# Sliding-window attention and MLP: splitting the W1 cast over two engines, centring rows without scaling in group 0, pacing GpSimd casts, spreading weight differences

## The chip, the cores and the metric

The kernel runs on one core of a Trainium2 chip. The metric is the device time of one launch in microseconds (us), as the median of several executions. A profile of one execution goes with each kernel; its span is about 2 us shorter than the measured time. Engine names in the profile: PE is TensorE (matmuls), PEld its weight loads, DVE is VectorE, ACT is ScalarE, POOL is GpSimd. "Lnnn" is a line of that kernel's own source, so the same operation has different line numbers before and after.

## The reference, cut to what matters

```python
def _attn_ref(q, k, v):                       # (8, 8, 576, 64), float32
    scores = (1 / sqrt(D)) * q @ k^T          # keys i-63 .. i of each query i only (window 64, causal)
    attn = softmax(scores)
    return attn @ v

def _moe_ref(x, g_ln, w_ch1, w_ch2):          # x: the attention result as (8, 576, 512)
    mu, var = mean(x), mean((x - mu)**2)      # over the 512 columns
    xn = (x - mu) / sqrt(var + 1e-06) * g_ln
    return x + relu(xn @ w_ch1) @ w_ch2       # 512 -> 2048 -> 512
```

## The kernel before

There are nine groups. Group g (0 to 7) is the first 512 rows of batch g; group 8 is the last 64 rows ("tails") of all eight batches. The MLP of group g is cut into about 30 "units" of TensorE work. After each unit the program emits what is listed for that slot: pieces of the attention of batch g+1 (scores, mask, product with v, row statistics, normalised rows z and their transpose zT), and the loads and casts of batch g+2. The order of emission is each engine's order of execution, so `at(u, f, ...)` sets where in each engine's queue the piece stands, but not when it runs.

GpSimd casts the inputs from fp32 to fp16. It has no data dependence on the MLP, so it runs a cast as soon as the input has landed and what stands before it in GpSimd's queue is done:

```python
    def cast_qk(b, half):
        for x in range(2):                    # q, then k: two casts of 128x1024 back to back
            ...
            nc.gpsimd.tensor_copy(out=dst..., in_=t...)
    def cast_v(b, c0, c1):
        nc.gpsimd.tensor_copy(out=vA[b][:, c0:c1, :, 0:D], in_=v32[b][:, c0:c1])
    def w1_cast(i):                           # 16 casts of 128x512 in all, g_ln folded in
        for c in range(2):
            nc.gpsimd.tensor_scalar(out=w1g[...], in0=t[:, c], scalar1=g4[:, kc:kc + 1], ..., op0=ALU.mult)
```

On VectorE, among others, are the mask, the normalised rows and the operands of layer 2, which from group 1 on is done by a scheme of seven block products instead of eight. It needs sums of activations in every group (`sw`) and eight differences of weights (`tw`, and two in place in `w2s`), which are computed once:

```python
    def s_mask(g, j):                         # two SBUF inputs, 128x1024
        nc.vector.tensor_tensor(out=ptv, in0=ptv, in1=mb, op=ALU.mult)
    def z_step(g, kb):                        # one SBUF input, fp32 -> fp16
        nc.vector.tensor_scalar(out=z, in0=x_norm..., scalar1=mv[:, 0:1], scalar2=rs[:, 0:1],
                                op0=ALU.subtract, op1=ALU.mult)
    def t_weights(i, c):                      # two SBUF inputs, 128x1024
        nc.vector.tensor_tensor(out=o, in0=a, in1=b, op=ALU.subtract)
```

The slots that matter here:

```python
        if g == 0:
            for n, i in enumerate((1, 2, 4)):           # six weight differences at the end of group 0
                for c in range(2):
                    at(26 + 2 * n + c, t_weights, i, c)
        else:
            if g == 1:
                at(0, t_weights, 3, 0); at(0, t_weights, 3, 1)      # (two lines in the source)
            ...
        if g > 1 and b < B:                             # attention of the next batch, b = g + 1
            for j in range(4):
                at(1 + 6 * j, s_mm, b, j); at(2 + 6 * j, s_mask, b, j)
                bz(7 + 6 * j, b, j); at(min(13 + 6 * j, 28), zt_step, b, j)
        if 0 < g and b + 1 < B:                         # loads and casts of the batch after it
            ...
            at(e + 8, cast_qk, n, 0)
            at(e + 10, cast_qk, n, 1)
            at(e + 16, cast_v, n, 0, 4)
```

The softmax here doesn't subtract the row's maximum and nothing guards it: scores larger than these inputs give would overflow.

## Time and profile before

The time is 346.97 us (346.14 to 348.06), the span of the profile 344.8 us. The table gives the stages. A stage begins at the first layer-1 matmul of its group in the timeline of PE, and the last one ends with the span. Busy time and granted clock are from the view of windows.

| stage before | from, us | length, us | PE busy, us | PEclk |
|---|---|---|---|---|
| start, to the first MLP matmul | 0 | 23.63 | | |
| group 0, layer 1 | 23.63 | 25.40 | 18.91 | 0.89 |
| group 0, layer 2 | 49.03 | 21.30 | 20.58 | 1.00 |
| group 1 | 70.33 | 49.40 | 38.53 | 0.90 |
| groups 2 to 5 | 119.73 | 127.93 | 123.41 | 1.00 |
| group 6 | 247.66 | 36.05 | 32.57 | 1.00 |
| group 7 | 283.71 | 29.59 | 29.59 | 1.00 |
| group 8 | 313.30 | 31.50 | 26.37 | 0.98 |

TensorE bounds the kernel nearly everywhere, so what counts is where PE waits. This is the view of PE's waits of the kernel before; the columns are: who waited <- for whom, us in total, times, longest.

```profile
PE hph L424 <- ACT hrT L429: 7.4, 1, 7.4
PE tp L216 <- POOL qk L126: 5.9, 2, 3.4
PE ztp L341 <- DVE z L330: 5.0, 8, 2.0
...
PE xps L307 <- DVE pt L291: 2.9, 3, 1.0
...
PE hph L424 <- POOL w1g L187: 2.1, 2, 1.3
```

The first line is one stall at the boundary of groups 0 and 1. The second contains one of 3.44 us in group 0: PE transposes q of batch 1, whose cast stands behind the W1 casts in GpSimd's queue. The timeline of GpSimd shows these (start, duration, engine, line, operation, tiles, shapes, count):

```profile
17.32 12.51 POOL L187 TENSOR_SCALAR w1g<-w1s,g 128x512 f16<-128x512 f32 x8 [0.77 <-DMA w1s<-in_moe_w_ch_dram]
29.82 12.34 POOL L187 TENSOR_SCALAR w1g<-w2s,g 128x512 f16<-128x512 f32 x8
42.11 2.01 POOL L126 CAST qk<-qk 128x1024 f16<-128x1024 f32 x2
```

The first wait of the list and the one for `pt` (the product with v waits for the mask, 2.9 us) have another cause, which two timelines show together. VectorE before:

```profile
69.76 6.08 DVE L371 TENSOR_TENSOR tw<-w2s,tw 128x1024 f16<-128x1024 f16 x3
...
186.70 5.05 DVE L291 TENSOR_TENSOR pt<-pt,mask 128x1024 f16<-128x1024 f16 x1 [2.64 <-ACT pt L278]
...
194.09 0.66 DVE L291 TENSOR_TENSOR pt<-pt,mask 128x1024 f16<-128x1024 f16 x1
```

GpSimd before, at the same times:

```profile
70.11 3.98 POOL L126 CAST qk<-qk 128x1024 f16<-128x1024 f32 x4
...
186.06 1.05 POOL L123 CAST qk<-qk 128x1024 f16<-128x1024 f32 x1
...
188.27 1.03 POOL L123 CAST qk<-qk 128x1024 f16<-128x1024 f32 x1
...
189.31 1.88 POOL L145 CAST vA<-v 128x2048 f16<-128x2048 f32 x1
```

The same mask multiplication takes 0.66 us at 194.09 and 5.05 us at 186.70, and the long one ends at 191.75, 0.56 us after the last cast that reads SBUF (189.31 + 1.88 = 191.19). Three weight differences take 6.08 us across the casts of 70.11. Operations with an input in PSUM keep their duration: all seven `xn` that overlap such a cast take 0.69 us, like the other 29. This is what the Trainium skill describes in "SBUF — State Buffer", section "Who interferes with whom": VectorE with two SBUF inputs and a GpSimd instruction that reads SBUF want the same read port, and the one that comes second stands still until the other is done. The mask before shows it with 5.05 us instead of 0.66.

### The profile page before, as it was taken

The page shows a single profiled execution, that of the slowest core. Times are in us where ns is not written, and L with a number is a line of the kernel's source. Part 1 is how long each engine was busy: PE and PEld are TensorE (multiplying, and loading weights), DVE is VectorE, ACT ScalarE, POOL GpSimd, SP SyncE. Part 2 cuts the span into 40 slices and gives each one's busy share as a digit, 9 for nine tenths or more (in the row PEclk, how much of TensorE's full clock was granted, in tenths as well). Part 3 has the DMA queues.
Part 4 walks back from the last instruction along what each step waited for, and adds up shares of the span by engine and source line. Part 5 has one row for each costly group of instructions (what it writes and reads, how often), then busy time and mean ns, then how long its engine had stood idle before and what let it go on. Part 6 is the DMA issues. An engine that isn't in the chain of part 4 may idle for free.

```text
span 344.8 us, 7486 instructions
## 1 busy us (share of the span) xinstructions
PE 306.4 (89%) x3093; PEld 201.3 (58%) x3093; DVE 228.0 (66%) x366; ACT 170.5 (49%) x340; POOL 120.2 (35%) x152
## 2 busy tenths in 40 slices
PE   4976699928979899998999899899999789999993
PEld 1545354416867745854684478358746664586483
DVE  0662066497789668859885897689558974872352
ACT  2484442504856477246536652673387227813600
POOL 6599985456340180046007300800223303001000
PEclk9989989976999999999999999999999999999999
DMA  8999449997199479939975894794197995003004
GB/s 181 281 381 267 172 145 283 308 195 234 41 224 231 110 179 223 204 124 154 238 155 167 167 243 96 190 184 72 64 209 141 153 195 131 2 2 122 0 2 122
DMA packets 119890, 56.82 MB, mean 165 GB/s; under 512 B 96080, under 2 KB 112976, under 8 KB 119856
## 3 DMA queue, kind: packets, MB, share of 16 engines
q1 hardware_dynamic: 115904, 45.10, 58.3%
q0 software_dynamic: 2976, 10.72, 9.8%
q10 hardware_dynamic: 976, 0.53, 0.6%
q8 instruction: 24, 0.39, 0.5%
q14 instruction: 10, 0.08, 0.1%
HBM read 38.80 MB, written 9.44 MB: 140 GB/s over the span
## 4 chain that ended last, share of the span: by engine, by line
PE 58%; DVE 17%; POOL 9%; DMA 6%; SPq 3%; ACT 3%; issue 2%; DVEq 0%; POOLq 0%
PE hps L393 24%; PE wX L464 13%; POOL w1g L187 6%; PE wZ L464 5%; DVE pt L291 5%; PE hph L424 4%; PE wY L464 4%; DMA qk<-in_k_dram 3%; PE xps L307 3%; PE sc L274 2%; DVE osb L481 2%; DVE sw L383 2%; SPq L139 2%; PE ztp L341 2%; DVE stats L315 2%
## 5 line engine op out<-in xcount | busy, mean ns | idle before, releaser
L393 PE MATMUL hps<-zT,w1g 128*128 128x512 f16 x480 | 111.3, 381 | 0.7 <-ACT zT L344 0.7
L397 ACT ACTIVATE hrT<-hps 128x512 f16<-128x512 f32 x120 | 71.8, 598 | 38.7 <-PE hps L393 37.3
L393 PEld LDWEIGHTS <-w1g 128*128 128x128 f16 x480 | 45.4, 98 | 53.6 <-issue 4.5
L354 POOL DMA_DIRECT2D out_dram<-osb x18 | 12.6, 697 | 154.0 <-DVE osb L481 143.5
L464 PEld LDWEIGHTS <-sw 128*128 128x128 f16 x512 | 48.7, 98 | 10.0 <-issue 3.2
L291 DVE TENSOR_TENSOR pt<-pt,mask 128x1024 f16<-128x1024 f16 x28 | 37.0, 1320 | 19.3 <-ACT pt L278 10.6
L344 ACT COPY zT<-ztp 128x512 f16<-128x512 f16 x36 | 20.9, 582 | 42.7 <-PE ztp L341 42.7
L464 PEld LDWEIGHTS <-hrT 128*128 128x128 f16 x384 | 37.1, 98 | 6.4 <-issue 0.7
L424 PE MATMUL hph<-zT,w1g 128*128 128x256 f16 x192 | 26.3, 291 | 10.4 <-ACT hrT L429 7.4
L383 DVE TENSOR_TENSOR sw<-hrT 128x1024 f16<-128x1024 f16 x32 | 22.7, 712 | 15.5 <-ACT hrT L397 15.5
L323 ACT ACTIVATE rs<-mv,epst 128x1 f32<-128x1 f32 x36 | 10.6, 295 | 38.4 <-DVE mv L317 38.4
L126 POOL CAST qk<-qk 128x1024 f16<-128x1024 f32 x24 | 25.0, 1050 | 9.1 <-PE tp L216 2.8
L424 PEld LDWEIGHTS <-w1g 128*128 128x128 f16 x192 | 19.0, 103 | 14.7 <-issue 8.6
L284 ACT ACTIVATE pt<-sc 128x512 f16<-128x512 f32 x40 | 21.7, 595 | 9.1 <-PE sc L274 8.2
L315 DVE BATCH_NORM_STATS2 stats<-xn 128x6 f32<-128x512 f32 x36 | 25.0, 695 | 1.2
L210 DVE COPY qkT<-tp 128x1024 f16<-128x1024 f16 x6 | 7.3, 1225 | 27.9 <-PE tp L216 27.9
L313 DVE TENSOR_TENSOR xn<-xps,rcp 128x512 f32<-128x512 f32 x36 | 24.9, 691 | 1.2
L481 DVE TENSOR_TENSOR osb<-wX,xn 128x512 f32<-128x512 f32 (+1 forms) x25 | 16.6, 664 | 11.1 <-PE wX L464 11.1
L330 DVE TENSOR_SCALAR z<-xn,mv,rs 128x512 f16<-128x512 f32 x36 | 21.3, 593 | 3.2 <-ACT rs L324 3.0
L145 POOL CAST vA<-v 128x512 f16<-128x512 f32 (+1 forms) x14 | 16.8, 1210 | 9.9 <-DMA v<-in_v_dram 9.7
L307 PEld LDWEIGHTS <-pt 128*64 128x64 f16 x576 | 12.5, 112 | 12.9 <-DVE pt L291 4.8
L429 ACT ACTIVATE hrT<-hph 128x512 f16<-128x512 f32 x24 | 14.3, 597 | 11.0 <-PE hph L424 10.9
(70 smaller groups left out, 445.7 us busy)
## 6 DMA issues: line engine op xcount, KB each, us to landing
qk<-in_q_dram SPq DMA_DIRECT2D x16, 512.0 KB, 6.2
v<-in_v_dram SPq DMA_DIRECT2D x32, 256.0 KB, 5.7
out_dram<-osb POOLq DMA_DIRECT2D x14, 512.0 KB, 3.2
w2s<-in_moe_w_ch_dram SPq DMA_DIRECT2D x12, 512.0 KB, 6.4
qk<-in_k_dram SPq DMA_DIRECT2D x8, 512.0 KB, 6.6
qk<-in_k_dram SPq DMA_DIRECT2D x16, 256.0 KB, 6.5
w1s<-in_moe_w_ch_dram SPq DMA_DIRECT2D x4, 512.0 KB, 6.6
tk<-in_k_dram SPq DMA_DIRECT2D x8, 256.0 KB, 4.3
```

Source lines behind the costliest of these rows:

```text
L126: nc.gpsimd.tensor_copy(out=dst[:, :].rearrange("p (a j) e d -> p a e j d", j=j), in_=t[:, :].rearrange("p (a e j d) -> p a e j d", e=2, j ...
L284: nc.scalar.activation(out=pt[:, par], in_=sc[par], func=AF.Exp, bias=0.0, scale=scale)
L291: nc.vector.tensor_tensor(out=ptv, in0=ptv, in1=mb, op=ALU.mult)
L307: nc.tensor.matmul(out=xps[64 * r:64 * r + 64, h, :D + 1], lhsT=pt[:, par, hp, r, :], rhs=rhs, start=True, stop=True)
L313: nc.vector.tensor_tensor(out=xn, in0=xps[:, :, 0:D], in1=rcp_b, op=ALU.mult)
L315: nc.vector.bn_stats(out=stats, in_=xn.rearrange("p h d -> p (h d)"))
L383: nc.vector.tensor_tensor(out=S[i], in0=a, in1=b, op=op)
L393: nc.tensor.matmul(out=hps, lhsT=w1g[:, kc, 128 * hc:128 * (hc + 1)], rhs=zT[g][:, kc, :], start=(kc == 0), stop=(kc == NKC - 1),)
L397: nc.scalar.activation(out=hrT[:, hc, :], in_=hps, func=AF.Relu, bias=0.0, scale=1.0)
L424: nc.tensor.matmul(out=hps[:, e], lhsT=w1g[:, kc, 128 * hc:128 * (hc + 1)], rhs=zT[g][:, kc, 256 * half:256 * half + 256], start=(kc == 0) ...
L464: nc.tensor.matmul(out=xyz[bank][:, t], lhsT=lhsT, rhs=rhs, start=bool(first and t == 0 and hc == 0), stop=(t == 1 and hc == 7), skip_grou ...
L481: nc.vector.tensor_tensor(out=o, in0=xyz[bank][:, ts], in1=x if base == "x" else o, op=ALU.add)
```

## The change

Its intent has five main parts.

1. Of the 16 W1 casts, GpSimd keeps 8 and ScalarE takes 8, so that GpSimd gets to the casts of batch 1 sooner.
2. Group 0 uses rows that are centred but not scaled by r = 1/sqrt(var + eps). As r is positive, relu(r·a) = r·relu(a), so r can be multiplied in at the end, in the addition to the output (`add_out`). That takes the ScalarE steps for r (`r_step`) off the path to the first MLP unit.
3. The eight weight differences move from the group boundary to one slot each in units 1 to 8 of group 1.
4. From group 2 on, each GpSimd cast is preceded by a tiny copy of one element per partition that reads a result of MLP unit u, or, for v, of the next batch's normalisation (the "pace" token), so that casts come one at a time, and the mask is emitted where no cast should be running. Scores, masks and tails get new slots.
5. In group 1, the shifted copy of v (`vB`) of batch 2 is made by two DMAs instead of by seven VectorE copies.

The diff holds more: layer 1 takes its four input chunks in the order 0, 2, 1, 3 (first those whose weights GpSimd casts), the casts of W2 and the loads after them are emitted only at unit 6 of group 0, the first blocks of group 0 are normalised and transposed in another order, and the casts of the tails are cut into three paced pieces.

The diff, cut to its core:

```diff
-    def w1_cast(i):
+    def w1_cast(i, c):
...
-            nc.gpsimd.tensor_scalar(out=w1g..., in0=t[:, c], scalar1=g4[:, kc:kc + 1], ..., op0=ALU.mult)
+        if c == 0:
+            nc.gpsimd.tensor_scalar(out=dst, in0=t[:, c], scalar1=g4[:, kc:kc + 1], scalar2=None, op0=ALU.mult)
+        else:
+            nc.scalar.activation(out=dst, in_=t[:, c], func=AF.Identity, bias=0.0, scale=g4[:, kc:kc + 1])
...
     def z_step(g, kb):
+        if g == 0:
+            nc.vector.tensor_scalar(out=z, in0=x, scalar1=mv[:, 0:1], scalar2=None, op0=ALU.subtract)
+        else: ...
+    def pace(t):
+        nc.gpsimd.tensor_copy(out=tok, in_=t)
...
         def add_out(kb):
-            nc.vector.tensor_tensor(out=o, in0=ch[kb], in1=x_norm..., op=ALU.add)
+            nc.vector.scalar_tensor_tensor(out=o, in0=ch[kb], scalar=rss[(g, kb)][:, 0:1],
+                in1=x_norm..., op0=ALU.mult, op1=ALU.add)
...
     TAILS = {
-        6: (... (10, s_mm, 8, 0), (11, s_mask, 8, 0), (16, b_step, 8, 0), (22, zt_step, 8, 0), ...
+        6: (... (11, s_mm, 8, 0), (12, s_mask, 8, 0), (17, b_step, 8, 0), (23, zt_step, 8, 0), ...
...
         if g == 1:
-            at(4, init_vB, 2)
+            at(4, alloc_vB, 2)
             at(5, cast_v, 2, 0, 4)
+            at(5, make_vB, 2)
-            for c in range(4):
-                at(7, vB_cur, 2, c, 1)
-                if c < 3:
-                    at(7, vB_prev, 2, c, 1)
...
-                at(0, t_weights, 3, 0)
-                at(0, t_weights, 3, 1)
+                for n, i in enumerate((1, 2, 4, 3)):
+                    for c in range(2):
+                        at(1 + 2 * n + c, t_weights, i, c)
...
             for j in range(4):
-                at(1 + 6 * j, s_mm, b, j)
-                at(2 + 6 * j, s_mask, b, j)
-                bz(7 + 6 * j, b, j)
-                at(min(13 + 6 * j, 28), zt_step, b, j)
+                at((0, 6, 11, 17)[j], s_mm, b, j)
+                at((1, 7, 12, 18)[j], s_mask, b, j)
+                bz((6, 11, 17, 23)[j], b, j)
+                at((12, 17, 23, 28)[j], zt_step, b, j)
...
+            if n < NPE:                       # batches 2 and 3 (cast in groups 0 and 1): as before, not paced
+                at(e + 8, cast_qk, n, 0)
+                at(e + 10, cast_qk, n, 1)
+                ...
+            else:
+                for u, x, half in ((3, 0, 0), (5, 1, 0), (8, 0, 1), (10, 1, 1)):
+                    at(u, lambda u=u: pace(hrTs[g][:, u, 0:1]))
+                    at(u, cast_q, n, x, half)
+                ...
+                for u, c, j in ((18, 0, 1), (20, 1, 2), (24, 2, 2), (26, 3, 3)):
+                    at(u, ... pace(...))
+                    at(u, cast_v, n, c, c + 1)
```

## The prediction

> **What bounds the kernel now.** TensorE: PE is busy 306.4 of the 344.8 us span (busy table), so about 38 us of PE idle is all there is to win, and some 15 us of it lies in the first 22 us (inputs arriving) and the last 5 us (stores), which the change hardly touches. The waits and the timeline of PE put the rest in four places.
>
> 1. Start, group 0. GpSimd casts W1 from 17.3 to 42.1 us: 16 casts of 1.56 us (timeline of GpSimd). PE waits 0.85 + 1.26 us for W1, 0.94 us for the zT copy, 3.44 us (39.6 to 43.2) for the q cast queued behind W1, and then runs at a lower granted clock (0.86).
> 2. Boundary of groups 0 and 1. Three weight differences on VectorE take 6.08 us from 69.8 (one alone 4.88, normally 0.68), because GpSimd casts q and k from 70.1 to 74.1. They delay the normalisation, ScalarE waits 8.36 us for its variance, PE waits 7.36 us. Granted clock afterwards 0.68 to 0.81.
> 3. Groups 2 to 5, period 32.24 us. The first mask multiply takes 4.0 to 5.05 us (0.69 elsewhere), until the GpSimd casts end (186.7 to 191.75 against 185.1 to 191.1). PE waits 0.98 us for it and 0.40 us for z at the end of each group.
> 4. Group 6 (36.1 us): waits of 2.28, 0.74 and 0.42 us.
>
> The Trainium skill, "SBUF — State Buffer", section "Who interferes with whom", says a VectorE instruction with two SBUF inputs contends with a GpSimd instruction that reads SBUF, and the later one fully blocks. The trace agrees: mask and weight differences stretch until the casts end, while operations with a PSUM input keep their 0.69 us.
>
> **What the change does, costed.**
> - W1: GpSimd keeps 8 casts (12.5 us, done near 30), ScalarE gets 8 at about 0.6 us each (its 128x512 passes take 0.58 to 0.60). ScalarE then limits the first eight MLP units (relu 0.6 + cast 0.6 against 0.87 of PE), so layer 1's second part starts only 1 to 2 us earlier; the 3.44 us stall and its cold clock vanish. Gain about 6.5 us.
> - Unscaled rows remove a 0.6 us wait per block at the start, which ScalarE's casts take back. About 0.
> - Weight differences spread: the 7.36 us stall and the cold clock after it vanish. Gain 8 us. One difference can still be caught by the casts (about 1 us, little on PE).
> - Pacing: one cast blocks VectorE for at most about 1 us, and the mask runs before the first cast. Gain 1.4 us x 4 groups, less new collisions: 5 us.
> - Tails in group 6: gain 2 to 3 us.
> The 2 us wait in group 1 (98.3 to 103, v cast against sums) isn't addressed.
>
> Sum: about 22 us, nearly all on PE's path. Predicted 324.5 us, 8 in 10 between 319 and 332. Chances: faster by over 2% 0.95, within 2% 0.04, slower 0.01.
>
> **What would show each step right.** GpSimd's last W1 cast ends near 30 us; no PE wait of 3 us on a q cast; layer 2 of group 0 starts near 42 to 43 us (49.0 before). No PE wait over 2 us at the group 0 to 1 boundary. Period of groups 3 to 5 near 31 us, no mask multiply over 1.8 us. Group 6 near 33.5 us.
>
> **What would make it wrong.** W2 and the next q, k, v arriving late, so that group 0 is limited by DMA; ScalarE's casts delaying its relus more than said; paced v casts delaying the vB copies; paced casts colliding with the pre-sums, so that periods stay near 32 us.

## The result, and the profile after

The changed kernel takes 331.71 us (330.8 to 332.5, four runs) against 346.97 us (346.14 to 348.06, four runs): ratio 0.956, 95% interval 0.952 to 0.960. Ratios here are the mean time of one kernel's fast runs over that of the other's of the same rounds, so not quite the ratio of the medians quoted. The time lies just inside the predicted range, but the gain is 15.2 us where 22 were expected. The stages, by the same definition as above:

| stage | before | after | difference | predicted |
|---|---|---|---|---|
| start | 23.63 | 21.95 | -1.68 | (in the next line) |
| group 0, layer 1 | 25.40 | 19.95 | -5.45 | -6.5 with the start |
| group 0, layer 2 | 21.30 | 21.28 | 0.0 | 0 |
| group 1 | 49.40 | 45.65 | -3.75 | -8 |
| groups 2 to 5 | 127.93 | 123.83 | -4.10 | -5 |
| group 6 | 36.05 | 34.98 | -1.07 | -2 to -3 |
| group 7 | 29.59 | 30.03 | +0.44 | 0 |
| group 8 | 31.50 | 32.03 | +0.53 | 0 |
| span | 344.8 | 329.7 | -15.1 | about -22 |

The view of PE's waits after:

```profile
PE tp L221 <- DVE qkT L215: 2.7, 1, 2.7
PE ztp L356 <- DVE z L342: 2.7, 4, 1.1
PE tp L221 <- POOL qk L131: 2.3, 1, 2.3
...
PE hph L440 <- ACT zT L359: 1.5, 1, 1.5
PE xps L312 <- DVE xn L318: 1.4, 1, 1.4
```

The 7.4 us wait and the wait for W1 are gone, and so is the wait of 3.4 us for a cast of q (what is left of that line, 2.3 us, is at the very start, while inputs arrive). The new head of the list is a single wait of 2.7 us in group 1. W1 in GpSimd's timeline after:

```profile
17.38 3.11 POOL L193 TENSOR_SCALAR w1g<-w1s,g 128x512 f16<-128x512 f32 x2 [0.79 <-DMA w1s<-in_moe_w_ch_dram]
21.60 3.27 POOL L193 TENSOR_SCALAR w1g<-w1s,g 128x512 f16<-128x512 f32 x2 [1.11 <-DMA w1s<-in_moe_w_ch_dram]
24.84 6.18 POOL L193 TENSOR_SCALAR w1g<-w2s,g 128x512 f16<-128x512 f32 x4
```

GpSimd is through with W1 at 31.0 instead of 42.2 us, and layer 2 of group 0 starts at 41.9 instead of 49.0. Each cast on ScalarE takes 0.71 to 0.72 us (0.6 had been estimated from passes that read PSUM).

Group 1 is where the prediction missed most. VectorE after:

```profile
64.89 2.10 DVE L342 TENSOR_SCALAR z<-xn,mv,rs 128x512 f16<-128x512 f32 x1
...
70.44 2.22 DVE L386 TENSOR_TENSOR tw<-w2s 128x1024 f16<-128x1024 f16 x1
72.59 0.58 DVE L342 TENSOR_SCALAR z<-xn,mv,rs 128x512 f16<-128x512 f32 x1
73.10 2.94 DVE L386 TENSOR_TENSOR tw<-w2s,tw 128x1024 f16<-128x1024 f16 x1
75.96 1.21 DVE L215 COPY qkT<-tp 128x1024 f16<-128x1024 f16 x1
...
142.47 0.69 DVE L296 TENSOR_TENSOR pt<-pt,mask 128x1024 f16<-128x1024 f16 x1 [1.84 <-ACT pt L283]
```

GpSimd after, at the same times:

```profile
62.19 3.98 POOL L131 CAST qk<-qk 128x1024 f16<-128x1024 f32 x4
...
70.23 1.89 POOL L150 CAST vA<-v 128x2048 f16<-128x2048 f32 x1 [2.39 <-DMA v<-in_v_dram]
...
73.47 2.02 POOL L131 CAST qk<-qk 128x1024 f16<-128x1024 f32 x2
...
144.71 0.70 POOL L348 CAST tok<-hrT 128x1 f32<-128x1 f16 x1 [2.73 <-ACT hrT L412]
145.35 1.04 POOL L131 CAST qk<-qk 128x1024 f16<-128x1024 f32 x1
```

One difference is held by the cast of v of batch 2 (until 72.1), another by the casts of q and k of batch 3 (until 75.5). The second one starts 0.37 us before these casts, while GpSimd still issues the DMAs of `vB` (72.42 to 73.47), so which of the two engines came first can't be read from this profile. Neither is a collision at the old place, the boundary; the spread operations met other casts, which are not paced. The copy `qkT`, which only reads PSUM and itself keeps its 1.21 us, stands behind the 2.94 us difference in VectorE's queue, and PE waits for that copy. PE after:

```profile
77.23 1.01 PE L221 MATMUL tp<-ident,qk 128*128 128x128 f16 x8 [2.73 <-DVE qkT L215]
78.03 3.82 PE L440 MATMUL hph<-zT,w1g 128*128 128x256 f16 x24
```

The 24 `hph` matmuls after the wait take 3.82 us, where the same 24 take 2.80 us in a run without it (pace_q3 below). The view of windows says why, in its column for the granted clock (0.50, then 0.81, after PE stood still; asked for 76.72 to 80.14 alone it gives 0.50):

```profile
77.20:79.00 1.80, 1.77 (x13) 1.52 (x13) 1.80 (x4) 0.72 (x1) 0.69 (x1) 0.50 1.08 171
79.00:82.00 3.00, 3.00 (x36) 2.29 (x35) 2.02 (x2) 1.60 (x4) 1.06 (x2) 0.81 0.96 154
```

(columns: window; its length, then busy us and instructions of PE, PEld, DVE, ACT, POOL; granted clock as a share of full speed; DMA share; GB/s).

In groups 3 to 5 the period is 30.97 us, as predicted; the first mask takes 0.69 us (142.47 above) and its cast waits for the token at 144.71. PE is busy for 123.20 of the 123.83 us of groups 2 to 5, 99.5%, so there is nothing more to win there by moving waits.

### The profile page after: what moved, and what is told of

Same layout as the page of the kernel before. It is cut to its first block, busy times and chain, and to the rows that moved or that the text cites. A ratio compares the mean times of both kernels' runs of the same rounds, so it can differ in the third digit from the quotient of the medians.

```text
span 329.7 us, 7565 instructions
## 1 busy us (share of the span) xinstructions
PE 303.8 (92%) x3093; PEld 200.2 (61%) x3093; DVE 206.5 (63%) x359; ACT 175.1 (53%) x348; POOL 127.2 (39%) x198
## 4 chain that ended last, share of the span: by engine, by line
PE 71%; DVE 12%; ACT 11%; issue 2%; DMA 2%; POOL 0%; DVEq 0%
PE hps L408 28%; PE wX L480 15%; PE wZ L480 8%; PE wY L480 3%; PE sc L279 3%; PE xps L312 3%; ACT pt L289 3%; PE hph L440 2%; DVE sw L398 2%; PE ch L420 2%; PE ztp L356 2%; ACT hrT L412 2%; DVE stats L320 2%; DVE xn L318 2%; PE tp L221 2%
## 5 line engine op out<-in xcount | busy, mean ns | idle before, releaser
L398 DVE TENSOR_TENSOR sw<-hrT 128x1024 f16<-128x1024 f16 x32 | 23.6, 741 | 21.2 <-ACT hrT L412 21.2
L296 DVE TENSOR_TENSOR pt<-pt,mask 128x1024 f16<-128x1024 f16 x28 | 19.7, 705 | 15.1 <-ACT pt L289 7.7
L315 DVE RECIPROCAL rcp<-xps 128x8 f32<-128x8 f32 x36 | 7.4, 205 | 26.8 <-PE xps L312 26.8
L348 POOL CAST tok<-hrT 128x1 f32<-128x1 f16 x25 | 10.1, 403 | 34.3 <-ACT hrT L412 29.9
L150 POOL CAST vA<-v 128x512 f16<-128x512 f32 (+1 forms) x26 | 19.3, 744 | 9.9 <-DMA v<-in_v_dram 9.7
L342 DVE TENSOR_SCALAR z<-xn,mv,rs 128x512 f16<-128x512 f32 x32 | 20.1, 632 | 0.8 <-ACT rs L332 0.6
```

Source lines behind the costliest of these rows:

```text
L342: nc.vector.tensor_scalar(out=z, in0=x, scalar1=mv[:, 0:1], scalar2=rss[(g, kb)][:, 0:1], op0=ALU.subtract, op1=ALU.mult)
L398: nc.vector.tensor_tensor(out=S[i], in0=a, in1=b, op=op)
```

## The experiments

All kernels gave correct results. Runs are in three sessions, each on a chip of its own and with its own runs of the kernel before (medians 348.04, 347.99 and 348.52 us); between sessions compare the ratios. Every one of these kernels is faster than the kernel before by over 2%, except e5 and e7, where the interval reaches across 2% and the verdict is unclear. e1 to e4 were profiled twice: the times read from timelines below are of the first profile, and where the kept second one differs it is given too. The changed kernel was run again as a control (c_after). Where an expectation names a theory by a letter, A is the blocking of VectorE by GpSimd casts that are not paced, B is that VectorE simply has too much work in group 1, C is that the tail block and batch 7 share units in group 6, and D the rivals of C.

### Control: the changed kernel again (c_after)

No edit.

> The changed kernel itself again, as a control on the same chip as the runs beside it. The first experiments showed group 1 at 41.4 us in one kernel and 45.7 us in another although both have the same code there, so one profile of group 1 is not a fixed number. If that is so (when the loads of v and of the next q and k land decides which weight difference meets which GpSimd cast), the runs of this kernel scatter over 3 us or more, around 330 to 333 us; if the kernel is steady, they agree within 1 us and group 1 is again 45.5 us.

Measured: 331.92 us, ratio 0.952 (0.947 to 0.956); its fast runs spread from 329.33 to 333.15, and one of 334.61 was counted as slow and left out (it is over 1.5% above the fastest, but its granted clock, 0.981, isn't below that of the others, 0.981 to 0.989, so it may belong to the same scatter). In the profile group 1 takes 46.36 us, with a PE wait of 3.96 us for the same copy. What follows: the runs scatter by over 3 us, as the first alternative says. The kernel before scatters as much in the same session (347.01 to 350.77, eleven runs), so this isn't new with the change, and a difference of 1 to 2 us between single runs means nothing here.

### Group 1: pacing the casts of batch 3 (e1_pace_q3)

```diff
-                at(e + 8, cast_qk, n, 0)
-                at(e + 10, cast_qk, n, 1)
+                for u, x, half in ((9, 0, 0), (11, 1, 0), (13, 0, 1), (15, 1, 1)):
+                    at(u, lambda u=u: pace(hrTs[g][:, 2 * (u % 8), 256 * (u // 8):256 * (u // 8) + 1]))
+                    at(u, cast_q, n, x, half)
```

> Edit: in group 1 alone, the four GpSimd casts of batch 3's q and k are paced to MLP units 9, 11, 13 and 15, instead of running as soon as GpSimd is free. Theory A (contention: the spread weight differences of group 1 wait out unpaced GpSimd casts that read SBUF, and the qkT copy behind them in VectorE's queue holds up PE): the third weight difference falls from 2.94 us to about 0.7, PE's 2.73 us wait for the qkT copy and the cold clock after it vanish, group 1 falls from 45.65 us to about 41.5 to 42.5, the time to about 328 us. Rival B (VectorE simply has 5.4 us more work ahead of that copy, so its queue is late whatever GpSimd does): the wait stays near 2.7 us, the time within 1 us of 331.7.

Measured: 328.74 us (328.3 to 329.06), ratio 0.944 (0.940 to 0.948). PE's wait for the copy falls from 2.73 to 0.31 us and the clock stays up (24 `hph` matmuls in 2.80 us). But group 1 only falls to 44.53 us (43.60 in the second profile), not to the expected 41.5 to 42.5: the cast of v of batch 3, now right after the paced casts (86.34, 2.16 us), holds a pre-sum for 2.51 us, and PE waits 1.77 us for a later pre-sum of the same queue and 1.13 us for a z. So the wait did come from the unpaced casts of q and k, and the next unpaced cast took its place.

### Group 1: the delayed copy on ScalarE instead (e2_copy_on_act)

```diff
-            at(4, t_main, 2, 0, 1, 1)
+            at(4, t_main, 2, 0, 1, 0)
```

> Edit: the third copy of transposed q out of PSUM in group 1 is made by ScalarE instead of VectorE; the GpSimd casts stay unpaced. Theory A's chain (blocked difference, then copy behind it, then PE): the difference stays at about 2.9 us, but PE no longer waits 2.73 us for the copy; group 1 gains 2 to 4 us, the time is about 328.5 to 330 us. If PE's wait came from somewhere else (late q cast, z of block 3), the wait of about 2.7 us stays and the time does not move by 1 us.

Measured: 328.17 us (326.96 to 329.44), ratio 0.943 (0.939 to 0.947); group 1 43.71 us (43.52 in the second profile). The difference is still blocked (2.94 us), but PE no longer waits for the copy. A wait of 2.54 us for a z appears later, behind a mask of 2.23 us that runs against the cast of v (84.05 to 85.94). What follows: the way the time reaches PE is the place of the copy in VectorE's queue; and again a later cast takes some of it back.

### Group 1: the differences back at the boundary (e3_weights_back)

```diff
+        if g == 0:
+            for n, i in enumerate((1, 2, 4)):
+                for c in range(2):
+                    at(26 + 2 * n + c, t_weights, i, c)
...
-                for n, i in enumerate((1, 2, 4, 3)):
-                    for c in range(2):
-                        at(1 + 2 * n + c, t_weights, i, c)
+                at(0, t_weights, 3, 0)
+                at(0, t_weights, 3, 1)
```

> Edit: the eight weight differences are put back where the kernel before has them (six at the end of group 0, two at the start of group 1); all else is as changed. Theory A: the 7 us PE stall at the boundary of groups 0 and 1 comes back, while group 1's new 2.7 us wait goes: group 1 is again about 48 to 50 us against 45.65, the time about 335 to 336 us. Rival (the gain of group 1 came from the vB copies that moved to DMA, not from spreading): the time stays within 1 us of 331.7.

Measured: 332.8 us (331.9 to 333.47), ratio 0.956 (0.952 to 0.960), against 0.956 and 0.952 of the changed kernel in its two sessions. The stall at the boundary is back (three differences in 6.08 us, PE waits 6.13 us), yet group 1 takes 47.04 us (46.03 in the second profile) against 45.65 and 46.36, and the time is near that of the rival and not the 335 to 336 us of theory A. So spreading the differences, which had been credited with 8 us, is by itself worth 0 to 1.5 us by these figures (the intervals of the ratios leave up to some 3.5 us open): it exchanged one collision for others. The other 2.4 to 3.4 us by which group 1 is shorter than the 49.40 us before are not traced to a part of the change; the rival's own reason, the `vB` copies, is tested in e10 below and finds no support.

### Group 1 cleared of casts (e9_g1_clear)

The casts of batch 2 move ahead (units 27 and 28 of group 0), the v cast of batch 2 waits until the differences are through, and all casts of batch 3 are paced.

```diff
-            at(30, cast_qk, 2, 0)
-            at(30, cast_qk, 2, 1)
+            at(27, cast_qk, 2, 0)
+            at(28, cast_qk, 2, 1)
...
-            at(5, cast_v, 2, 0, 4)
-            at(5, make_vB, 2)
+            at(7, lambda: pace(hrTs[1][:, 14, 0:1]))
+            at(7, cast_v, 2, 0, 4)
+            at(7, make_vB, 2)
...
-                at(e + 8, cast_qk, n, 0)     # and the other casts of batch 3
+                for u, x, half in ((9, 0, 0), (11, 1, 0), (13, 0, 1), (15, 1, 1)): ... pace(...); at(u, cast_q, n, x, half)
+                for u, c, t in ((22, 0, ...), (24, 1, ...), (26, 2, ...), (28, 3, ...)): ... pace(t()); at(u, cast_v, n, c, c + 1)
```

> Edit, all in what GpSimd does around group 1: the casts of batch 2's q and k run at units 27 and 28 of group 0 (before the third store instead of after it), v of batch 2 is cast after unit 7 of group 1, batch 3's q and k after units 9, 11, 13, 15, and its v in four paced pieces at units 22 to 28. VectorE's own work is unchanged. Theory A (the loss in group 1 is weight differences and z waiting out GpSimd casts): the eight differences take 0.68 us each, PE's waits in group 1 fall from 7.6 us to about 2, group 1 falls to 40.5 to 41.5 us, and the runs scatter less; about 4 us less than the control. Rival B (VectorE has too much work in group 1): group 1 stays over 44 us.

Measured: 328.3 us (327.28 to 328.56, six runs), ratio 0.942 (0.938 to 0.945), that is 3.6 us below the control of the same session, with a spread of 1.3 us against the control's 3.8. The view of the tile `tw` shows the durations in ns (min/median/max):

```profile
L386 DVE TENSOR_TENSOR tw<-w2s,tw x4: 684/686/687, 71.8 to 74.7; 128x1024 f16<-128x1024 f16 x4
L386 DVE TENSOR_TENSOR tw<-w2s x2: 681/686/691, 69.0 to 70.7; 128x1024 f16<-128x1024 f16 x2
```

All are undisturbed, the two in place in `w2s` too (687 ns), with no less VectorE work than in the changed kernel (only the casts on GpSimd moved). So A is confirmed and B falls. Group 1 still takes 42.64 us, because this kernel made itself a new wait: the v cast after unit 7 is late, and PE waits 2.51 us for the DMA that makes `vB` from it.

### Group 1: vB by VectorE copies again (e10_vb_copies)

```diff
-            at(4, alloc_vB, 2)
+            at(4, init_vB, 2)
-            at(5, make_vB, 2)
+            for c in range(4):
+                at(7, vB_cur, 2, c, 1)
+                if c < 3:
+                    at(7, vB_prev, 2, c, 1)
```

> Edit: batch 2's shifted copy of v (vB) is again made by seven VectorE copies in group 1 instead of two DMAs; the weight differences stay spread. With the weights put back, group 1 was still 47.0 us against 49.4 before, so part of its gain may be these copies (4.0 us of VectorE work). If so: group 1 is 48 us or more, the time 2 to 4 us over the control's 331.9. If they are not on the path: within 1 us of the control.

Measured: 328.8 us (328.05 to 329.0, six runs), ratio 0.943 (0.940 to 0.946); group 1 41.85 us. The expectation failed: the kernel with more VectorE work is about 3 us faster than the changed one (0.943 against 0.952) and steadier. This also speaks against B. Why it is faster isn't settled. In its trace GpSimd doesn't issue the two DMAs (0.53 us each), and the casts of batch 3 come one by one, as the loads and the transposes release them; the longest difference of the first three takes 1.52 us. But its casts also happened to begin earlier, at 60.32 us against 62.19, and the unchanged group 1 takes 41.42 us in a profile where they begin at 60.32 too (e4 below). So the one profile doesn't tell whether the copies or the start made the difference; six runs within 1 us say only that it isn't one lucky run.

### How much of group 1 is chance

The code of group 1 is the same in seven kernels with eight profiles (e4 was profiled twice). The second row tells by how much the casts of q and k of batch 2 begin before the first matmul of group 1:

| kernel | after | control | e4 | e4 again | e5 | e6 | e7 | e8 |
|---|---|---|---|---|---|---|---|---|
| group 1, us | 45.65 | 46.36 | 41.42 | 47.54 | 43.11 | 47.01 | 47.52 | 42.48 |
| casts begin earlier by, us | 1.0 | 1.2 | 3.1 | -0.8 | 3.2 | 0.5 | -0.8 | 3.9 |

In the changed kernel an addition to the output at 60.6 us waits 2.71 us for a store to free its buffer, the casts of q and k start at 62.19, and v of batch 2 has landed only by 70.23. In e4_tail_moved the casts start at 60.32, v is there by 67.49, and the casts of q and k of batch 3 meet the differences elsewhere: the longest of the first three takes 1.44 us. The two profiles of e4 are two executions of one kernel. GpSimd and VectorE in the first:

```profile
60.32 3.98 POOL L131 CAST qk<-qk 128x1024 f16<-128x1024 f32 x4
...
73.43 0.68 DVE L386 TENSOR_TENSOR tw<-w2s,tw 128x1024 f16<-128x1024 f16 x1
```

and in the second, where the addition to the output waits 4.67 us for a store and PE waits 2.72 us for the copy again:

```profile
63.10 3.98 POOL L131 CAST qk<-qk 128x1024 f16<-128x1024 f32 x4
...
73.88 2.94 DVE L386 TENSOR_TENSOR tw<-w2s,tw 128x1024 f16<-128x1024 f16 x1
```

So what group 1 costs, some 6 us of it, goes with when the casts begin, and they stand behind the stores in GpSimd's queue. That the landing of stores and loads is the cause was not tested by itself. e9, which moves and paces these casts, spread over 1.3 us; e12 below, which does nearly the same, has one run of six that is 3 us off, so the steadiness isn't settled either.

### Groups 2 to 5: no pacing (e5_no_pace)

```diff
     def pace(t):
-        nc.gpsimd.tensor_copy(out=tok, in_=t)
+        pass
```

> Edit: the pacing reads are taken out; casts, pieces and units stay. GpSimd then starts the casts of q and k as soon as the stores are issued, about 1 us into groups 2 to 5, in front of or during the first mask multiply. Theory E (pacing is what keeps the mask free): the first mask multiply is again 3 to 5 us, PE waits 1 us or more for it in each of four groups (the product now comes a unit earlier, so up to 2 us), periods go from 30.97 to 32 to 33 us, time 4 to 8 us over the control. Rival F (the new units of scores and masks are enough): periods stay at 31 us.

Measured: 340.44 us (338.4 to 340.7), ratio 0.976 (0.971 to 0.980), 8.5 us above the control; periods of groups 2 to 5 of 32.55, 33.6, 33.6 and 34.6 us. VectorE and GpSimd in this run:

```profile
143.26 6.31 DVE L296 TENSOR_TENSOR pt<-pt,mask 128x1024 f16<-128x1024 f16 x1 [1.78 <-ACT pt L283]
...
147.31 2.73 POOL L150 CAST vA<-v 128x512 f16<-128x512 f32 x4
```

The mask of 6.31 us ends at 149.57; the casts run from 142.76, with short memsets in between, to 150.04. PE waits 2.25 us for this mask. Without pacing the new slots are worse than the old kernel's 32.24 us.

### Groups 2 to 5: pacing at the old slots (e6_old_slots)

```diff
-                at((0, 6, 11, 17)[j], s_mm, b, j)
-                at((1, 7, 12, 18)[j], s_mask, b, j)
-                bz((6, 11, 17, 23)[j], b, j)
-                at((12, 17, 23, 28)[j], zt_step, b, j)
+                at(1 + 6 * j, s_mm, b, j)
+                at(2 + 6 * j, s_mask, b, j)
+                bz(7 + 6 * j, b, j)
+                at(min(13 + 6 * j, 28), zt_step, b, j)
...
-                for u, c, j in ((18, 0, 1), (20, 1, 2), (24, 2, 2), (26, 3, 3)):
+                for u, c, j in ((20, 0, 1), (22, 1, 2), (26, 2, 2), (28, 3, 3)):
```

> Edit: pacing stays, but scores, masks, products and transposes of groups 2 to 6 go back to their old units (1, 7, 13, 19 and so on); the v pieces move two units later where their token isn't there yet. The run without pacing had periods of 33.6 us at the new units, the kernel before 32.24 at the old ones. If pacing alone gains the 0.98 us and the new units the 0.40 us for z, periods are 31.3 to 31.4 us against 30.97, and group 6, where tail and main blocks no longer share units, falls from 35 to 33.5 us or less; time within 1.5 us of the control. If the new units carried the gain, periods are 32 us or more.

Measured: 335.29 us (331.92 to 335.81), ratio 0.960 (0.955 to 0.965); periods of 31.2 us. The expectation for the time, within 1.5 us of the control, failed: by the ratios it is 2.8 us above, with group 1 again at the long end (47.01 us) and group 6 longer. The periods decide: of the 1.27 us that a period lost (32.24 to 30.97), pacing at the old slots gives 1.04 and the new slots then 0.23; PE's wait of 0.40 us for the last z of a group is still there with the old slots and gone with the new. The expectation for group 6 failed (36.31 us): the tail block's scores now stand alone, but wait 1.84 us for the transposing DMA of the tail's k; why that lands too late here was not looked into.

### Group 6: the tail block moved (e4_tail_moved)

```diff
-        6: (... (11, s_mm, 8, 0), (12, s_mask, 8, 0), (17, b_step, 8, 0), (23, zt_step, 8, 0),
+        6: (... (14, s_mm, 8, 0), (15, s_mask, 8, 0), (20, b_step, 8, 0), (26, zt_step, 8, 0),
```

> Edit: in group 6 the first tail block's scores, mask, product and transpose move from units 11, 12, 17, 23 to 14, 15, 20, 26, so that they no longer share units 11 and 17 with a block of batch 7. Theory C (two score steps in one unit exceed the two score buffers in PSUM, two product steps the one product buffer): PE's waits of 0.98 us for the exponential, 1.42 us for xn and 0.29 us in group 6 vanish, group 6 falls from 34.98 us to about 32.5, the time to about 329.5 us. Rival D (tail casts colliding with VectorE cause them): waits stay, group 6 stays within 0.5 us of 35.

In the changed kernel, PE's timeline has these waits in group 6:

```profile
246.21 0.19 PE L279 MATMUL sc<-tqT,tkT 64*128 64x64 f16 x1 [0.68 <-ACT pt L283]
...
255.26 0.45 PE L312 MATMUL xps<-vt,pt 128*64 128x65 f16 x16 [1.42 <-DVE xn L318]
```

The scores of the tail block and of batch 7's third block both stand at unit 11, and their products with v both at unit 17; each needs a buffer that the other has just filled. Measured with the block moved: none of these waits is left, and group 6 falls from 34.98 to 32.81 us. C is shown. Group 7 takes 30.72 us instead of 30.03, so 1.5 us is left of the 2.2; the second profile has 32.60 and 30.31 us and none of the waits either. The time is 328.04 us (325.92 to 330.75), ratio 0.943 (0.939 to 0.948); part of that is the short group 1 of its runs (41.42 us in the profile), so the verdict rests on the stage and not on the total.

### Start: W1 all on GpSimd, rows unscaled (e7_w1_all_pool)

```diff
-        if c == 0:
+        if True:                             # and all 16 casts in the old order, before batch 1
```

> Edit: all sixteen W1 casts on GpSimd again, in the old order; unscaled rows and all else as changed. If the split is what gained 7.1 us before layer 2 of group 0, that layer starts again near 48 to 49 us and the time is 6 to 7 us over the control. If the unscaled rows carry part of the gain, layer 2 starts at 46 us or earlier.

Measured: 340.95 us (338.33 to 343.23), ratio 0.978 (0.973 to 0.984). That is 9.0 us over the control, more than the 6 to 7 expected; in its profile group 1 is at the long end too (47.52 us). Layer 1 starts at 20.76, and layer 2 at 47.81 us. PE waits four times for W1, 4.6 us in all, and again for the cast of q of batch 1:

```profile
28.57 0.39 PE L440 MATMUL hph<-zT,w1g 128*128 128x256 f16 x2 [0.91 <-POOL w1g L193]
30.11 1.59 PE L440 MATMUL hph<-zT,w1g 128*128 128x256 f16 x13 [1.15 <-POOL w1g L193]
...
43.43 0.62 PE L221 MATMUL tp<-ident,qk 128*128 128x128 f16 x8 [3.46 <-POOL qk L131]
```

### Start: W1 split, rows scaled as before (e8_scaled_rows)

```diff
-        if g == 0:                           # in z_step
+        if False:
...
-            nc.vector.scalar_tensor_tensor(out=o, in0=ch[kb], scalar=rss[(g, kb)][:, 0:1], in1=x_norm..., ...)
+            nc.vector.tensor_tensor(out=o, in0=ch[kb], in1=x_norm..., op=ALU.add)
...
+    r_step(0, 0)                             # likewise for the other blocks, each right before its z_step
```

> Edit: group 0 again on rows scaled by the inverse deviation (its two ScalarE steps stand between variance and z, as before), W1 still split. The prediction said the unscaled rows are worth about 0. With W1 all on GpSimd the unscaled rows started layer 1 at 20.76 us against 23.63 us, which says they may be worth more. If about 0: layer 2 of group 0 starts at 41 to 42 us as in the control and the time is within 1 us of 331.9. If they matter: layer 1 starts near 23.5 instead of 22, layer 2 near 43 to 44, the time is 1.5 to 3 us over the control.

Measured: 333.97 us (331.89 to 335.05), ratio 0.957 (0.953 to 0.961). Layer 1 starts only at 26.65 us, and layer 2 at 47.74:

```profile
26.65 1.88 PE L439 MATMUL hph<-zT,w1g 128*128 128x256 f16 x8 [1.07 <-ACT zT L359]
```

This start isn't wholly that of the scaling. The edit doesn't restore the old order of the blocks: in the kernel before, the copy of zT of block 1 stands in front of the r step of block 2, here behind it. ScalarE:

```profile
25.60 0.29 ACT L331 ACTIVATE rs<-mv,epst 128x1 f32<-128x1 f32 x1 [2.13 <-DVE mv L322]
25.92 0.20 ACT L332 ACTIVATE rs<-rs 128x1 f32<-128x1 f32 x1
26.03 0.57 ACT L359 COPY zT<-ztp 128x512 f16<-128x512 f16 x1
```

The transpose that this copy waits for is done at 24.19 us (23.58 + 0.61), so up to some 1.8 us of e8's late start comes from this order (an estimate from these times).

The two runs, each with one profile, complete a table of the start of layer 2 of group 0:

| | W1 all on GpSimd | W1 split |
|---|---|---|
| rows scaled | 49.03 (before) | 47.74 (e8) |
| rows unscaled | 47.81 (e7) | 41.90 and 41.11 (after, control) |

Each part alone gives 1.2 to 1.3 us, both together 7.1 us or more. Two reservations: with the old order of blocks the split alone might give up to some 3 us, and the cell "before" differs from the other three also in the untested parts named under the change. That the two parts need each other still holds: with W1 split the unscaled rows are worth 5.8 us or more, less at most 1.8. With the rows scaled, ScalarE has the r steps, which wait 1.21 and 2.13 us for statistics, the exponentials and its W1 casts in one queue before layer 1 can begin; with W1 on GpSimd alone, layer 1 begins earliest of all and then waits for W1 and for q. The total of e8 is only some 2 us above the control's, by the ratios, as its group 1 was among the short ones (42.48 us).

### All findings together (e12_best)

The slots of e9 with the v cast of batch 2 paced at unit 5 instead of 7, the tail block of e4, and ScalarE's second half of W1 casts one unit later, so that zT comes before them:

```diff
-                at(3 + j, w1_cast, 4 + j, 1)
+                at(4 + j, w1_cast, 4 + j, 1)
...
+            at(5, lambda: pace(hrTs[1][:, 10, 0:1]))
```

> The changed kernel with three edits: GpSimd's casts around group 1 moved and paced as in the run that cleared group 1, but v of batch 2 after unit 5, since after unit 7 PE waited 2.5 us for its shifted copy; the tail block of group 6 at units of its own; ScalarE's last four W1 casts one unit later, behind the copy of zT that PE waited 1.55 us for. Expected: group 1 about 40.5 us, group 6 32.8 us, layer 1 of group 0 0.5 us shorter, together 6 to 8 us under the control: 323.5 to 326 us, with runs within 1.5 us of each other.

Measured: 326.44 us (325.21 to 330.0, six runs), ratio 0.938 (0.933 to 0.942): it beats both the kernel before and the changed one. Against e9 (0.938 to 0.945, another session) the intervals overlap. The expectation failed, narrowly in the time (323.5 to 326) and clearly in group 1 and the scatter: group 1 takes 42.73 us, no better than in e9, and one run of 330.0 us shows that it isn't quite steady. Group 6 takes 33.15 us, as expected, and the wait for zT in group 0 is 0.94 us instead of 1.55. GpSimd and VectorE in group 1:

```profile
72.77 3.01 POOL L348 CAST tok<-hrT 128x1 f32<-128x1 f16 x1 [6.20 <-ACT hrT L445]
75.73 1.89 POOL L150 CAST vA<-v 128x2048 f16<-128x2048 f32 x1
...
72.65 1.89 DVE L386 TENSOR_TENSOR tw<-w2s,tw 128x1024 f16<-128x1024 f16 x3
74.45 1.29 DVE L386 TENSOR_TENSOR w2s<-w2s 128x1024 f16<-128x1024 f16 x2
```

The token, which takes 0.19 us when undisturbed, took 3.01 us: it started 0.12 us after a train of five differences and ended with them at 75.8. The lock works in the other direction too, so the v cast was as late as in e9, and PE waited 2.56 us for the DMA of `vB`.

## Why the prediction was right or wrong, point by point

- **Total: right direction, gain too large.** 331.71 us lies inside 319 to 332, at its edge, by 0.3 us where runs scatter by over 3, so that it fell inside is partly luck. The sum of terms, 22 us, was 15.1 us in the profile.
- **"GpSimd's last W1 cast ends near 30 us; layer 2 of group 0 starts near 42 to 43 us": right** (31.0 and 41.9), and so is the size (7.1 us against 6.5). **The attribution was wrong.** The prediction gave it all to the split and "about 0" to the unscaled rows. The table above shows that each needs the other for most of the gain, so the right size is luck too: it was credited to one part and came from two. The rows' small wait is not what they buy; by e8's timeline they take the r steps, and ScalarE's waits for them, out of the queue just where the split puts its casts.
- **"Weight differences spread: the 7.36 us stall and the cold clock after it vanish. Gain 8 us": the failed step.** The stall at the boundary did vanish in the changed kernel, but group 1 gained 3.75 us, and in e3 only 0 to 1.5 us of this is the spreading. The sentence "one difference can still be caught by the casts (about 1 us, little on PE)" was wrong in both halves: two were caught, for 2.22 and 2.94 us, and PE waited 2.73 us and then ran at half clock. What was missed is that casts of batches 2 and 3 aren't paced in this change, and that a PSUM copy which never collides itself stands behind a difference that does. e9 shows that with the casts moved every difference keeps its 0.69 us. How much the casts take in group 1 also changes from execution to execution: 41.42 and 47.54 us in the two profiles of e4.
- **"Pacing ... 5 us": mechanism right, size nearly.** Masks 0.69 us in groups 2 to 5, periods 30.97 us as predicted, 4.1 us in all. e6 shows that pacing gives 1.04 of the 1.27 us of a period at the old slots, and e5 that the new slots without it lose time.
- **"Tails in group 6: gain 2 to 3 us": mis-sized**, 1.07 us. The new slots put two score blocks and two products into one unit each; e4 shows that 2.2 us more was there, of which group 7 takes 0.7 back (2.4 and 0.3 in the second profile).
- **Groups 7 and 8** lost 0.44 and 0.53 us that the prediction didn't have; no run was spent on these.
- **Named risks:** "paced v casts delaying the vB copies" did not happen in the changed kernel, but did in e9 and e12, 2.5 us each. "ScalarE's casts delaying its relus" was small: one wait of 1.55 us for zT, of which 0.6 us went with one unit of shift. The other two didn't come about: in layer 2 of group 0 PE is busy for 20.60 of 21.28 us, and the periods are as predicted.

## What to carry to other kernels

When an operation that two engines block each other on is moved, list every operation of the other engine that the new place can meet, the ones the change did not touch included, and look at what stands behind it in its own queue: that is how the time gets to the bottleneck. Pace an engine that runs ahead by data of the bottleneck engine, and look at every part that is left unpaced: here one stage of it took 41.42 us in one execution of a kernel and 47.54 in another. Test two parts of a change that share an engine both alone and together, since here each alone was worth 1.2 to 1.3 us, or up to 3 with the old order of blocks, and both 7. When an edit takes a part back, check that it takes back the order too. Profile a kernel twice before reading a stage of it.

## What the Trainium skill lacked or had wrong

- "SBUF — State Buffer", section "Who interferes with whom": agreed with in kind. A VectorE operation with two SBUF inputs was held by GpSimd's casts, and `z`, a `tensor_scalar` with one SBUF input, which the page says can contend, took 2.10 us instead of 0.55. It says that the later one blocks for the whole instruction of the other. The runs show more: VectorE waited for a whole train of GpSimd casts of at most 1.9 us each (mask of 5.05 us before, 6.31 us in e5), and a GpSimd copy of one element per partition waited 3.01 us for a train of five VectorE operations of 0.69 us (e12).
- The same section has no advice on pacing. In groups 2 to 5 it was worth 1.04 us in a period of 32.24, and leaving it out at the new slots cost 8.5 us in all.
- "TensorE: Matmul & The Clock Gate", section "What's actually happening", has the clock throttle after at least one idle window of about 3.4 us. Here the granted clock was 0.50 for 3.4 us at or after waits of 2.73 us (after, from 76.72 us) and 2.51 us (e9, from 84.42 us), so a single wait need not be 3.4 us long; in the changed kernel 24 matmuls then took 3.82 instead of 2.80 us. The length of the wait doesn't decide alone: the same wait of 1.77 us in e1 was followed by 0.55 in one profile and by 1.00 in the other, and of three waits of 2.25 us in e5 only the last was followed by 0.50. What decides isn't shown.
- No page has that such collisions make the time vary from run to run: group 1 of one kernel (e4) took 41.42 us in one profile and 47.54 in another. That the collisions make the totals scatter is not shown: the changed kernel's fast runs spread over 3.8 us and e9's, without these collisions, over 1.3, but e12's, without them too, over 4.8.
